# Attention, Fourier mixing and feed-forward on one core: first-half statistics moved up, loads untied, single events shifted by a table

## The chip, the cores and the metric

The kernel runs on one core of a Trainium2 chip. The metric is device time in microseconds (us) from launch to the end of the program. The kernel before has a median of 1042.02 us over three runs (1040.59 to 1042.19). The engines are named as in the profile: PE (TensorE matmul), PEld (its weight loads), DVE (VectorE), ACT (ScalarE), POOL (GpSimd), SP (the engine that issues most DMAs).

## The reference

```python
scores = scale * q @ k^T                       # 8 batches, 8 heads, 576 rows, 64 wide
scores = where(0 <= i - j < 128, scores - slope[h] * |i - j|, -1e9)
attn   = softmax(scores);  x = attn @ v        # heads side by side: 576 x 512 a batch
u      = x + real(fft(fft(x, axis=1), axis=2)) # over the 576 rows and the 512 columns
un     = (u - mean(u)) / sqrt(var(u) + 1e-6)   # over the 512 columns
out    = u + relu(un @ w_ch1) @ w_ch2          # 512 -> 2048 -> 512
```

All is to be right to float32; the two weight matrices come as 8-byte words, which the kernel turns into pairs of float16 itself.

## The kernel before, in words

**Tiling.** The work runs over 32 head pairs p (four a batch). A pair has 576 queries in five tiles, of which each sees one or two blocks of 128 keys; the tiles form three column groups i = 0, 1, 2 (`SGRP`). `products` (L668) makes the scores of a group, with 64-row matmuls of both heads side by side; `spread` adds slope and mask and takes the row minimum on DVE (L684); ACT takes the exponential. In batches 0 and 1 (`NF = 2`) P is turned by PE (`turn`, L715) and multiplied in float32 with v (`values`, L737); from batch 2 on all operands are split in two float16 parts (`convert`, `halves`), P is turned by DMA (`flip`, L706) and each product takes three matmuls (L742 to L744). `weigh` (L756 to L760) divides by the row sums and writes a head's 64 columns of X. There is one `pv` buffer, so a head's `values` wait for the `weigh` of the head before.

**Behind a batch's eight heads** comes `fourier`: rows of X are folded on DVE (L807 to L859), multiplied with cosine tables on PE (`rows` L871, `middle` L888, `cols` L905, three column blocks j in the order 1, 0, 2), and added into X on DVE (`cols_add`, L923 to L934). Then `norm` takes mean and variance (L978, L979), a power on POOL (L981), the shift `nmr` (L983), the normalized rows in two parts (L990, L991 and the difference, L424 `un`), and a DMA transpose into uT. It is called for two halves (X[0:2], X[2:4]) and, for odd batches, a rest. `ffn` is a generator: the first layer (L1151) and relu (L1156), then the second (L1173); each of its `yield`s is one step. The last batch has a variant with fewer products (L1088).

**Beside this** run the weights: loads of 512 KB, two exponent and bit steps (`rebias` L452, `join` L457, L458), a Gram matrix on PE for the scale (L466), and the split into high (ACT, L484) and low (DVE, L488) parts. For batches 2 to 7 `batch_scales` loads q, k and v once more in pieces of up to 256 KB (`fetch`, L528) and squares them on ACT (`part`, L535) for the scale. A one-element POOL copy before the load (L527) reads the X that the last `weigh` wrote, so the load can't go before it; another (L534) ties `part` to the pace of the relu.

**What sets the order.** `put(t, f, ...)` files an event at a time t that is a formula of hand-set numbers (`LB`, `SA`, `F0`, ...). The events run in order of t and emit instructions. `collect` groups these and finds what each waits for, `arrange` plays them through a model with one queue an engine (among the ready ones the first emitted goes first) and `keep_order` writes the resulting order of each engine into the program. So an engine's order is fixed when the program is built.

In the order listings below sp_N are score banks and turned blocks (N is a buffer number), `wall` the weights, `un` the normalized rows. The lines of `norm`'s statistics and of the tie are:

```python
            if b > NF:
                G.tensor_copy(box[x][1][0:1, 0:1], last[-1])   # L527
            nc.sync.dma_start(out=box[x][1], in_=fl[:, o:o + n])  # L528
        for i, t1 in enumerate((t - f * 0.1, t + f * 0.7)):
            put(t1, norm, b, lambda i=i: st["X"][2 * i:2 * i + 2], t + f * (0.9 + 1.6 * i))
```

Of the kernel before, what the change touches and what calls it, by code (L numbers as in the profile page):

```python
# [22 lines left out]
NF = 2  # L23
# [29 lines left out]
SPIN, GAP = 5, 1.315  # L53
# [29 lines left out]
WIDTH = {"float32": 4, "float16": 2, "bfloat16": 2, "int32": 4, "int64": 8}  # L83
LANES = ("PE", "DVE", "Activation", "Pool", "SP")
# [28 lines left out]
def cells(a, seen):  # L113
# [4 lines left out]
    if b.tensor.name[:2] in ("fp", "sp", "pv", "pd"):  # L118
        return b.tensor.name, 0, 128, 1
# [16 lines left out]
def nanoseconds(i, lane):  # L136
# [34 lines left out]
def collect(traced):  # L171
    work, seen, last = [], {}, -1
    for at, i in enumerate(traced):
# [8 lines left out]
        if it is None or bank is None or it.bank != bank or last != at - 1 or len(it.ins) >= 24:  # L182
            it = Work(lane, form, bank)
            work.append(it)
# [10 lines left out]
    writes, reads = {}, {}  # L195
    for n, it in enumerate(work):
        for (t, p0, p1, bits), w in it.uses:
            for l, real in ((writes, True),) + (((reads, False),) if w else ()):
                for m, q0, q1, other in l.get(t, ()):
                    if m != n and q0 < p1 and p0 < q1 and bits & other:  # L200
                        it.waits[m] = it.waits.get(m, False) or real
# [10 lines left out]
def arrange(work, slots):  # L212
# [31 lines left out]
    while len(order) < len(work):  # L244
        best = None
        for e in LANES:
            while now[e] or later[e]:
                t = free[e] if now[e] else max(free[e], later[e][0][0])
                while later[e] and later[e][0][0] <= t:
                    heappush(now[e], heappop(later[e])[1])  # L250
                n = now[e][0]
                t1, tag = buffers(n)
                if t1 is None:
                    held.setdefault(tag, []).append(heappop(now[e]))
                elif t1 > t:
                    ready[n] = max(ready[n], t1)
                    heappush(later[e], (ready[n], heappop(now[e])))
# [5 lines left out]
        n = heappop(now[e])  # L263
# [32 lines left out]
        for m, real in it.then:  # L296
            same = work[m].lane == e
            ready[m] = max(ready[m], end if same and (e == "PE" or not real and e != "SP") else seen + WAKE[work[m].lane])
# [14 lines left out]
def keep_order(tc, slots):  # L313
# [6 lines left out]
    order, takers = arrange(work, slots)  # L320
# [15 lines left out]
def attn_fft_ffn_kernel(  # L336
# [83 lines left out]
    def put(t, f, *a):  # L420
        heappush(queue, (t, next(order), f, a))
# [91 lines left out]
    def batch_scales(b, t0, dt):  # L513
# [6 lines left out]
        def fetch(x, fl, o, n):  # L520
# [5 lines left out]
            if b > NF:  # L526
                G.tensor_copy(box[x][1][0:1, 0:1], last[-1])  # L527
# [263 lines left out]
    def fourier(b, t0):  # L791
# [161 lines left out]
        for j in (1, 0, 2):  # L953
# [10 lines left out]
    def norm(b, of, t1):  # L964
# [7 lines left out]
        uTs[b].append(uT)  # L972
        ag = small.tile([128, 4, 2], F32, name="ag")
        rstd = small.tile([128, 4], F32, name="rstd")
        nmr = small.tile([128, 4], F32, name="nmr")
# [7 lines left out]
        put(t1 - 0.5 * f, lambda: V.scalar_tensor_tensor(nmr[:, :n], ag[:, :n, 0], -1.0, rstd[:, :n], ALU.mult, ALU.mult))  # L983
        uns = {}

        def scaled(i):
            t = t2k.tile([128, 1032], F32, name="un", tag="a4", bufs=3)
            un, both = t[:, 0:512], t[:, 512:1024].bitcast(F16)
            s, o = rstd[:, i:i + 1], nmr[:, i:i + 1]
# [223 lines left out]
    def step(g, t, dt):  # L1213
        if next(g, g) is not g:
            steps[0] += 1
            t += dt + (E0 if steps[0] == 16 else 0.0)
            put(t, step, g, t, dt)

    for b in range(B):
        t = begin_of(4 * b)  # L1220
        if b >= NF:
            batch_scales(b, *((t - SA, SD) if b == NF else (t - SB, SE)))
        fourier(b, transform_of(b))
        n = 80 if b % 2 else 64
        t = forward_of(b)
        put(t, step, ffn(b), t, (24 if b else forward_of(1) - t - E0) / n)
    for f in range(8):
        put(begin_of(4 * B) + 5 + 2.0 * f, combos, f)
    weights(0, W1A, W1D, W1B, W1E)
    weights(1, W2A, W2D, W2B, W2E)  # L1230
    while queue:
        now[0], _, f, a = heappop(queue)
# [115 lines left out]
```

## Time and profile before

| | |
|---|---|
| median of the runs | 1042.02 us |
| the profiled execution | 1041.73 us, its span 1039.9 us |
| PE, DVE, ACT, POOL busy | 1006.7, 761.8, 609.9, 73.3 us |
| mean granted clock of PE | 0.990 |
| DMA | 117.86 MB, mean 113 GB/s, 397 GB/s at most in one of 40 slices |

The page divides the span of 1039.9 us into 40 slices of 26 us. PE is busy 90% or more in nearly all of them; in slices 4 and 5 (78 to 130 us) it has 7 tenths and its granted clock 8 tenths. DVE has 9 and 8 tenths there. The first two slices move 365 and 397 GB/s, and most of the weights. A row with an idle time in brackets names the instruction that ended the engine's wait.

### The profile page before, as it was taken

The page shows a single profiled execution, that of the slowest core. Times are in us where ns is not written, and L with a number is a line of the kernel's source. Part 1 is how long each engine was busy: PE and PEld are TensorE (multiplying, and loading weights), DVE is VectorE, ACT ScalarE, POOL GpSimd, SP SyncE. Part 2 cuts the span into 40 slices and gives each one's busy share as a digit, 9 for nine tenths or more (in the row PEclk, how much of TensorE's full clock was granted, in tenths as well). Part 3 has the DMA queues.
Part 4 walks back from the last instruction along what each step waited for, and adds up shares of the span by engine and source line. Part 5 has one row for each costly group of instructions (what it writes and reads, how often), then busy time and mean ns, then how long its engine had stood idle before and what let it go on. Part 6 is the DMA issues. An engine that isn't in the chain of part 4 may idle for free.

```text
span 1039.9 us, 24569 instructions
## 1 busy us (share of the span) xinstructions
PE 1006.7 (97%) x9352; PEld 730.7 (70%) x9352; DVE 761.8 (73%) x2211; ACT 609.9 (59%) x1438; POOL 73.3 (7%) x243
## 2 busy tenths in 40 slices
PE   8997799899999999999999999999999999999998
PEld 5785585575767677675767677676767776858886
DVE  5898867986784768778784768779684848987451
ACT  7897967676745566567655566667444532445230
POOL 0000001100210012000000012000000000010000
PEclk9998899999999999999999999999999999999999
DMA  9953517656553366534863376434532230011000
GB/s 365 397 187 95 127 34 197 165 105 152 148 135 87 83 154 145 142 77 121 170 136 90 81 157 146 139 80 103 111 93 33 58 70 11 11 35 39 21 3 30
DMA packets 191511, 117.86 MB, mean 113 GB/s; under 512 B 154400, under 2 KB 164128, under 8 KB 191392
## 3 DMA queue, kind: packets, MB, share of 16 engines
q1 hardware_dynamic: 190816, 114.84, 43.9%
q8 instruction: 73, 1.20, 0.5%
q10 hardware_dynamic: 576, 1.45, 0.4%
q14 instruction: 46, 0.38, 0.1%
HBM read 70.63 MB, written 9.44 MB: 77 GB/s over the span
## 4 chain that ended last, share of the span: by engine, by line
PE 66%; DVE 6%; DMA 3%; ACT 2%; issue 1%; POOL 0%; SPq 0%; ACTq 0%; DVEq 0%; POOLq 0%
PE fp L1151 28%; PE fp L1173 25%; PE fp L1088 4%; PE sp L668 3%; DMA pt<-P 2%; PE pd L871 2%; PE pd L905 1%; PE pv L742 1%; PE pv L744 1%; PE pv L743 1%; DVE hbuf L424 1%; DVE P L684 1%; DMA qr<-q_dram 0%; DVE P L424 0%; PE pd L888 0%
## 5 line engine op out<-in xcount | busy, mean ns | idle before, releaser
L1151 PEld LDWEIGHTS <-wall 128*128 128x128 f16 x3840 | 338.8, 98 | 46.2 <-issue 7.9
L1151 PE MATMUL fp<-uT,wall 128*128 128x256 f16 x3072 | 356.1, 273 | 4.5 <-DVE hbuf L424 4.0
L1173 PE MATMUL fp<-wall,hbuf 128*128 128x512 f16 x1536 | 349.1, 379 | 0.7 <-DVE hbuf L424 0.7
L1173 PEld LDWEIGHTS <-hbuf 128*128 128x128 f16 x1536 | 143.6, 98 | 161.0 <-issue 3.1
L1156 ACT ACTIVATE hbuf<-fp 128x512 f16<-128x512 f32 x144 | 85.0, 591 | 186.7 <-PE fp L1151 186.7
L424 DVE SCALAR_TENSOR_TENSOR hbuf<-fp,hbuf 128x512 f16<-128x512 f32 x144 | 98.7, 686 | 95.0 <-ACT hbuf L1156 94.4
L424 ACT ACTIVATE P<-P,nb 128x256 f32<-128x256 f32 x320 | 132.3, 477 | 13.8 <-DVE nb L684 8.2
L684 DVE CUSTOM_DVE_ANT_0 P<-sp,rg,nsl 128x256 f32<-128x256 f32 x240 | 96.2, 448 | 20.8 <-PE sp L668 15.4
L424 DVE SCALAR_TENSOR_TENSOR P<-P 128x256 f16<-128x256 f32 x240 | 83.0, 389 | 22.2 <-ACT P L697 21.6
L697 ACT ACTIVATE P<-P 128x256 f16<-128x256 f32 x240 | 80.7, 385 | 22.4 <-DMA pt<-P 18.7
L668 PE MATMUL sp<-kk,qq 64*128 64x256 f16 (+5 forms) x880 | 77.3, 287 | 4.1 <-DVE kk L424 3.0
L535 ACT ACTIVATE wall<-wall 128x512 f32<-128x512 f32 (+2 forms) x90 | 54.1, 601 | 35.6 <-DMA wall<-k_dram 17.5
L742 PE MATMUL pv<-vhs,pt 128*128 128x65 f16 x432 | 53.9, 195 | 3.9 <-DMA pt<-P 1.9
L743 PE MATMUL pv<-vl,pt 128*128 128x64 f16 x432 | 53.9, 193 | 0.0
L744 PE MATMUL pv<-vhs,pt 128*128 128x65 f16 x432 | 53.8, 193 | 0.0
L742 PEld LDWEIGHTS <-pt 128*128 128x128 f16 x432 | 41.3, 98 | 16.1 <-issue 4.6
L737 PE MATMUL pv<-vr,pt 128*128 128x65 f32 x288 | 40.7, 281 | 5.6 <-DVE X L760 5.1
L743 PEld LDWEIGHTS <-pt 128*128 128x128 f16 x432 | 40.4, 99 | 7.5
L1151 PE MATMUL fp<-wall,wall 128*128 128x128 f16 x768 | 45.0, 219 | 0.0
L737 PEld LDWEIGHTS pv<-vr,pt 128*128 128x128 f32 x288 | 37.9, 200 | 8.8 <-issue 7.1
L668 PEld LDWEIGHTS <-qq 64*128 64x128 f16 (+1 forms) x720 | 31.1, 99 | 15.4 <-issue 11.7
L744 PEld LDWEIGHTS <-pt 128*128 128x128 f16 x432 | 40.6, 97 | 0.0
(230 smaller groups left out, 1380.5 us busy)
## 6 DMA issues: line engine op xcount, KB each, us to landing
qr<-q_dram SPq DMA_DIRECT2D x32, 304.0 KB, 4.0
hbuf<-w_dram SPq DMA_DIRECT2D x16, 512.0 KB, 8.7
out_dram<-X SPq DMA_DIRECT2D x32, 256.0 KB, 2.2
wall<-v_dram SPq DMA_DIRECT2D x30, 256.0 KB, 3.0
vr<-v_dram SPq DMA_DIRECT2D x24, 320.0 KB, 3.7
kr<-k_dram SPq DMA_DIRECT2D x24, 289.0 KB, 4.4
wall<-q_dram SPq DMA_DIRECT2D x24, 256.0 KB, 3.3
wall<-k_dram SPq DMA_DIRECT2D x24, 256.0 KB, 3.0
```

The source lines that it names most:

```text
L424: put(now[0] + dt, lambda: f(*a, **kw))
L535: A.activation(t, t, AF.Square, accum_out=box["mx"][:, i, c:c + 1])
L668: T.matmul(sp[e][:m, col:col + n], qq[h, c0:c0 + m], keys(kk[h], ti), start=(x == 0), stop=(x == len(prods) - 1))
L684: V.tensor_tensor_reduce(pt[:m, 0:n], sp[e][:m, col:col + n], tab[:m, pc:pc + n], mul, 3.0e38, ALU.add, ALU.min, nb[:m, ti:ti + 1])
L697: A.activation(hi, P32, AF.Copy, scale=2.0 ** 14)
L737: T.matmul(pv[:, ti], pt[:, col:col + 128], ops[p][2][:, e, vc], start=first, stop=last)
L742: T.matmul(pv[:, ti], ph, vh[:, e, vc], start=first, stop=False)
L743: T.matmul(pv[:, ti, 0:D], ph, vl[:, e, vc], start=False, stop=False)
L744: T.matmul(pv[:, ti], pl, vh[:, e, vc], start=False, stop=last)
L1151: T.matmul(fp[:, i * n:(i + 1) * n], w1_ap(e, c, f), uT[:, j, c, 0:n], start=(c == 0 and p == 0), stop=(c == 3 and p == 2))
L1156: A.activation(ht[:, 0], fp, AF.Relu)
L1173: T.matmul(op, hh[f][:, a, i * 128:(i + 1) * 128], w2_ap(e, f), start=(f == 0 and p == 0), stop=(f == 15 and p == 2))
```

## The change

Six things. (1) `norm` of the first half is filed behind the second of the three column blocks instead of behind the third, and the times of both halves' scaling get numbers of their own (`N1`, `N2`, `N3`); `nmr` is allocated when it is written. (2) The POOL copy ahead of `fetch` goes, for batches 3 to 7. (3) `arrange` no longer takes the first emitted of the ready ones but the one with the smallest time mark, where the mark is the event's time plus an entry of the table `LATER` (some 80 entries, by the name of the event; plus is later). (4) `collect` also waits where two engines read one PSUM bank, and where instructions of one engine use a tile that another took first. (5) Some 20 of the hand-set numbers move. (6) Feed-forward steps get names, so that the table can speak of them.

```diff
-WL = (-2.569, 0.042)
+WL = (-2.569, -0.036)
-FL, SA, SD, SB, SE = 1.9, 16.181, 0.696, 24.041, 1.166
+FL, SA, SD, SB, SE = 1.9, 16.181, 0.696, 26.459, 1.05
-START = 47.844
+START = 47.9
-SLOW = 1.476
-W2A, W2D, W2B, W2E = 13.895, 0.615, 21.285, 0.518
-W1D, W1B, W1E = 0.379, 11.116, 0.977
-F0 = 5.97
+SLOW = 1.301
+W2A, W2D, W2B, W2E = 14.377, 0.733, 21.018, 0.518
+W1D, W1B, W1E = 0.385, 11.436, 1.124
+F0 = 5.578
+N1, N2, N3 = 1.853, -0.15, 4.606
+LATER = {
+    "W1.load.0": 0.6, "W0.rebias.1": 0.3, "scores.(0,2)+1": 0.15, "W0.gram.2": 1.3, "turn.0.0.0+1": -13.5,
...
+}
-DS, D0 = 1.0, 12
+DS, D0 = 0.505, 12
...
-            for l, real in ((writes, True),) + (((reads, False),) if w else ()):
+            for l, real in ((writes, 2), (reads, 1)):
                 for m, q0, q1, other in l.get(t, ()):
+                    if real == 1 and not w and (work[m].lane == it.lane or t[:2] not in BANKS):
+                        continue
...
-                    heappush(now[e], heappop(later[e])[1])
-                n = now[e][0]
+                    n = heappop(later[e])[1]
+                    heappush(now[e], (rank_of[n], n))
+                n = now[e][0][1]
...
-            if b > NF:
-                G.tensor_copy(box[x][1][0:1, 0:1], last[-1])
             nc.sync.dma_start(out=box[x][1], in_=fl[:, o:o + n])
...
             t += f * 0.8
+            if j < 1:
+                put(t - f * 0.1, norm, b, lambda: st["X"][0:2], t + f * N1)
-        for i, t1 in enumerate((t - f * 0.1, t + f * 0.7)):
-            put(t1, norm, b, lambda i=i: st["X"][2 * i:2 * i + 2], t + f * (0.9 + 1.6 * i))
+        put(t + f * N2, norm, b, lambda: st["X"][2:4], t + f * N3)
...
-        now[0], _, f, a = heappop(queue)
+        now[0], _, here[0], f, a = heappop(queue)
+        marks.append((len(tc.nc.cur_bb.bb.instructions), now[0] + LATER.get(here[0], 0.0), here[0]))
         f(*a)
```

What this does to the orders is shown at three places. The changed kernel's lines stand some 40 further on: its L726 is L684, L532 is L488, L798 to L802 are L756 to L760, L965 to L976 are L923 to L934, L1021 and L1022 are L978 and L979, L468 is the helper L424.

**First place: DVE, around the fold of batch 0, before.** sp_1123 and sp_1124 are the scores of pair 4, group 2; L801 to L859 are the fold, which began nine rows higher up, behind the eighth head's X.

```order
L808 TENSOR_TENSOR fg<-X 128x512
L851 TENSOR_SCALAR stack_104<-pm,sc 33x1
L488 SCALAR_TENSOR_TENSOR wall_109<-wall_109,misc 128x1024
L850 SCALAR_TENSOR_TENSOR stack<-abcd,sc,stack 33x512
L852 SCALAR_TENSOR_TENSOR stack_104<-pm,sc,stack_104 33x1
L684 ISA P,nb<-sp_1123,rel_sb 128x256
L684 ISA nb 128x1
L817 TENSOR_TENSOR pm<-fg 128x2x256
L818 TENSOR_TENSOR pm<-fg 128x2x256
L858 TENSOR_SCALAR a_1054<-pm,sc 128x1
L684 ISA P,nb<-sp_1124,rel_sb 128x256
```

The same scores (here sp_1105 and sp_1106) in the changed order, with the eighth head's X (L802) and the first row of the fold (L843):

```order
L726 ISA P,nb<-sp_1105,rel_sb 128x256
L726 ISA nb 128x1
L726 ISA P,nb<-sp_1106,rel_sb 128x256
L726 ISA nb 128x1
L502 SCALAR_TENSOR_TENSOR wall_110<-X,wall_110 128x512
L532 SCALAR_TENSOR_TENSOR wall_109<-wall_109,misc 128x1024
L798 TENSOR_SCALAR ri<-pv 128x5
L801 RECIPROCAL ri<-ri 128x5
L802 TENSOR_TENSOR X<-pv,ri 128x5x64
L843 MEMSET X 1x512
```

The two spreads stood behind the first part of the fold and now stand ahead of the whole of it. Three weight splits (L488) that stood between X and the fold's last row now stand behind that row.

**Second place: DVE, statistics of batch 0, before,** from the second column block's last addition (L927) on.

```order
L927 TENSOR_TENSOR X<-X,ds 128x512
L978 BN_STATS st<-X 128x6
L923 TENSOR_TENSOR ds<-ab 33x257
L924 TENSOR_TENSOR ds<-ab 33x256
L931 TENSOR_TENSOR ds<-ab 32x257
L930 TENSOR_TENSOR X<-X,ds 1x512
L932 TENSOR_TENSOR ds<-ab 32x255
L933 TENSOR_TENSOR ut<-X,ds 32x512
L934 TENSOR_TENSOR ut<-X,ds 32x512
L979 BN_AGGR ag<-st 128x2
L978 BN_STATS st<-X 128x6 x2
L979 BN_AGGR ag<-st 128x2
```

The same place in the changed order:

```order
L969 TENSOR_TENSOR X<-X,ds 128x512
L1021 BN_STATS st<-X 128x6 x2
L1022 BN_AGGR ag<-st 128x2
L965 TENSOR_TENSOR ds<-ab 33x257
L1022 BN_AGGR ag<-st 128x2
L966 TENSOR_TENSOR ds<-ab 33x256
L1023 TENSOR_SCALAR rstd<-ag 128x2
L973 TENSOR_TENSOR ds<-ab 32x257
L972 TENSOR_TENSOR X<-X,ds 1x512
L974 TENSOR_TENSOR ds<-ab 32x255
L975 TENSOR_TENSOR ut<-X,ds 32x512
L976 TENSOR_TENSOR ut<-X,ds 32x512
```

Both statistics of the first half now stand ahead of the third block, and the second half's, which followed at once, come 26 rows further down.

**Third place: DVE, around the second k split of batch 2's pairs (kk) beside the fold of batch 1, before,** from the seventeenth head's X on.

```order
L760 TENSOR_TENSOR X<-pv,ri 128x5x64
L684 ISA P,nb<-sp_2460,rg,nsl 128x256
L684 ISA nb 128x1
L684 ISA P,nb<-sp_2460,rg,nsl 96x256
L684 ISA nb 96x1
L817 TENSOR_TENSOR pm<-fg 128x2x256
L818 TENSOR_TENSOR pm<-fg 128x2x256
L856 SCALAR_TENSOR_TENSOR fl_2498<-abcd,sc,fh_2455 128x512
L828 TENSOR_TENSOR abcd<-pm 128x2x128 x2
L858 TENSOR_SCALAR a_2500<-pm,sc 128x1
L424 SCALAR_TENSOR_TENSOR vl<-vr,sc,vhs 128x640
L859 SCALAR_TENSOR_TENSOR a_2500<-pm,sc,a_2500 128x1
```

The next row there is the kk split. The same place in the changed order, where sp_2466 is the same group of scores:

```order
L802 TENSOR_TENSOR X<-pv,ri 128x5x64
L726 ISA P,nb<-sp_2466,rg,nsl 96x256
L726 ISA nb 96x1
L468 SCALAR_TENSOR_TENSOR P<-P 128x128
L468 SCALAR_TENSOR_TENSOR kk<-kr,sc,kk 128x578
L468 SCALAR_TENSOR_TENSOR X<-fp,misc,X 128x512
```

Between X and the kk split stood eleven rows, five of them of the fold and one the v split; now there are three, none of them of the fold.

## Rows read from the trace of the kernel before

**Rows 1.** Page: busy us (share) xinstructions.

```profile
PE 1006.7 (97%) x9352; PEld 730.7 (70%) x9352; DVE 761.8 (73%) x2211; ACT 609.9 (59%) x1438; POOL 73.3 (7%) x243
```

**Rows 2.** Stretches: start:end us, busy us (instructions) by engine, PEclk, DMA share, GB/s.

```profile
78.00:84.00 6.00, 1.51 (x4) 0.79 (x4) 5.94 (x16) 3.42 (x7) 0.21 (x2) 0.69 0.00 0
84.00:90.00 6.00, 6.00 (x24) 3.68 (x24) 6.00 (x15) 3.50 (x7) 0.10 (x1) 0.50 0.00 0
...
114.00:120.00 6.00, 3.80 (x18) 3.52 (x19) 5.51 (x21) 6.00 (x10) 0.69 (x1) 0.53 0.44 92
```

**Rows 3.** Timeline of PE: start us, us, operation, [idle before <-what ended it].

```profile
82.01 0.69 PE L715 MATMUL sp<-ident,P 128*128 128x128 f32 x2 [4.03 <-ACT P L424]
...
115.56 1.51 PE L737 MATMUL pv<-vr,pt 128*128 128x65 f32 x6 [4.62 <-DVE X L760]
...
121.66 6.86 PE L1151 MATMUL fp<-uT,wall 128*128 128x256 f16 x48
```

**Rows 4.** Timeline of DVE, 70 to 132 us.

```profile
71.27 0.47 DVE L760 TENSOR_TENSOR X<-pv,ri 128x320 f32<-128x320 f32 x1
...
80.98 0.42 DVE L684 CUSTOM_DVE_ANT_0 P<-sp,rel_sb 128x256 f32<-128x256 f32 x1
81.33 0.08 DVE L684 DVE_READ_ACCUMULATOR2_ANT nb<- 128x1 f32 x1
...
86.47 1.27 DVE L488 SCALAR_TENSOR_TENSOR wall<-wall,misc 128x1024 f16<-128x1024 f32 x1
87.66 0.74 DVE L856 SCALAR_TENSOR_TENSOR fl<-abcd,sc,fh 128x512 f16<-128x512 f32 x1
...
99.63 0.42 DVE L684 CUSTOM_DVE_ANT_0 P<-sp,rel_sb 128x256 f32<-128x256 f32 x1 [2.93 <-PE sp L668]
...
110.92 1.25 DVE L978 BATCH_NORM_STATS2 st<-X 128x6 f32<-128x512 f32 x2
...
116.52 0.69 DVE L424 TENSOR_TENSOR un<-un 128x512 f16<-128x512 f32 x1
```

**Rows 5.** Timeline of PE, 96 to 104 us.

```profile
99.53 0.60 PE L715 MATMUL sp<-ident,P 96*128 96x96 f32 x4
99.98 0.56 PE L737 MATMUL pv<-vr,pt 128*128 128x65 f32 x4
100.37 0.25 PE L580 MATMUL pv<-pt 128*128 128x184 bf16 x1
```

**Rows 6.** Waits of PE from 122 us on: us in total, times, longest.

```profile
PE fp L1151 <- DVE hbuf L424: 4.0, 6, 1.5
PE sp L668 <- DVE kk L424: 3.0, 2, 2.4
PE pv L742 <- DMA pt<-P: 1.9, 2, 1.1
```

**Rows 7.** Timeline of DVE, 185 to 200 us.

```profile
188.77 0.48 DVE L760 TENSOR_TENSOR X<-pv,ri 128x320 f32<-128x320 f32 x1
...
193.56 0.81 DVE L424 SCALAR_TENSOR_TENSOR kk<-kr,sc,kk 128x578 f16<-128x578 f32 x1
```

**Rows 8.** Timeline of PE, 264 to 278 us.

```profile
263.82 2.13 PE L1151 MATMUL fp<-uT,wall 128*128 128x256 f16 x18
265.88 0.88 PE L668 MATMUL sp<-kk,qq 64*128 64x256 f16 x10
...
269.82 5.41 PE L1151 MATMUL fp<-uT,wall 128*128 128x256 f16 x48
275.06 0.19 PE L742 MATMUL pv<-vhs,pt 128*128 128x65 f16 x1
```

**Rows 9.** DMA issues: xcount, KB each, median us to landing; of all issues.

```profile
wall<-v_dram SPq DMA_DIRECT2D x30, 256.0 KB, 3.0
...
pt<-P SPq DMA_TRANSPOSE x240, 2.4
```

**Rows 10.** Waits of SP over the whole span.

```profile
SPq L528 <- POOL wall L527: 52.0, 21, 10.3
```

More of the change, by code (lines that the diff above doesn't have):

```diff
@@ L1 @@
+from bisect import bisect_right
 from contextlib import ExitStack
@@ L183, in collect @@
             it = Work(lane, form, bank)
+            it.at = at
             work.append(it)
@@ L209, in collect, with arrange @@
     return work
-def arrange(work, slots):
+def arrange(work, slots, rank_of):
     left, room, turn, taken, takers, rank = {}, {}, {}, set(), {}, {}
@@ L262, in arrange @@
         s, e = best
-        n = heappop(now[e])
+        n = heappop(now[e])[1]
         it = work[n]
@@ L297, in arrange @@
             same = work[m].lane == e
-            ready[m] = max(ready[m], end if same and (e == "PE" or not real and e != "SP") else seen + WAKE[work[m].lane])
+            at_end = same and (e == "PE" or not real or real == 1 and e != "SP")
+            ready[m] = max(ready[m], end if at_end else seen + WAKE[work[m].lane])
             open_[m] -= 1
@@ L319, in keep_order @@
     work = collect(list(tc.nc.cur_bb.bb.instructions))
-    order, takers = arrange(work, slots)
+    starts = [0] + [m[0] for m in marks]
+    times = [-1.0e9] + [m[1] for m in marks]
+    order, takers = arrange(work, slots, [times[bisect_right(starts, it.at) - 1] for it in work])
     last = {}
@@ L418, in attn_fft_ffn_kernel, with put @@
     now = [0.0]
-    def put(t, f, *a):
-        heappush(queue, (t, next(order), f, a))
+    scope, here, seen, marks = [""], [""], {}, []
+    def put(t, f, *a, name=None):
+        base = here[0] + "+" if here[0] else scope[0] + f.__name__ + "".join(
+            "." + str(x).replace(" ", "") for x in a if type(x) in (int, tuple))
+        base = name or base
+        seen[base] = seen.get(base, 0) + 1
+        key = base + str(seen[base]) if base.endswith("+") else base if seen[base] == 1 else f"{base}#{seen[base]}"
+        heappush(queue, (t, next(order), key, f, a))
     def after(dt, f, *a, **kw):
@@ L972, in norm @@
         uTs[b].append(uT)
+        nmr = []
         ag = small.tile([128, 4, 2], F32, name="ag")
         rstd = small.tile([128, 4], F32, name="rstd")
-        nmr = small.tile([128, 4], F32, name="nmr")
         for i, t in enumerate(tiles):
@@ L982, in norm, with shifts @@
         f = 1 if b else PACE[1]
-        put(t1 - 0.5 * f, lambda: V.scalar_tensor_tensor(nmr[:, :n], ag[:, :n, 0], -1.0, rstd[:, :n], ALU.mult, ALU.mult))
-        uns = {}
+        def shifts():
+            nmr.append(small.tile([128, 4], F32, name="nmr"))
+            V.scalar_tensor_tensor(nmr[0][:, :n], ag[:, :n, 0], -1.0, rstd[:, :n], ALU.mult, ALU.mult)
+        put(t1 - 0.5 * f, shifts)
         def scaled(i):
@@ L1216, in step @@
             t += dt + (E0 if steps[0] == 16 else 0.0)
-            put(t, step, g, t, dt)
+            put(t, step, g, t, dt, name=f"step{steps[0]}")
     for b in range(B):
```

30 lines of the change are left out of this document (20 added, 10 removed), and 19 rows, old and new, of the table LATER.

## The prediction

> **What bounds the kernel now.** I read the page's busy shares first. PE is busy for 1006.7 of 1039.9 us [rows 1], so at most 33 us of idle time can go, and nothing that merely relieves another engine is worth anything unless PE waits for it there. Next the table of stretches. Behind 130 us PE is full nearly everywhere; the hole is at 78 to 126 us, where PE has 1.51 us of work in one six-microsecond stretch and 3.80 in another. There the granted clock is 0.69, 0.50 and 0.53, that is 1.2 GHz for part or all of the stretch, while DVE is busy for 5.94, 6.00 and 5.51 of 6 us [rows 2]. So DVE sets the pace there, and its order decides when PE gets its operands.
>
> The timeline of PE then names the two waits in the hole: 4.03 us for an exponential, 4.62 us for the X of a head [rows 3]. The timeline of DVE says why. The eighth head's X ends at 71.74; the spread whose exponential PE wants starts only at 80.98, behind the first part of the fold and weight splits of 1.27 us; the fold's last row starts at 87.66 [rows 4]. Up to the second `un` at 116.52, on which the first feed-forward matmul at 121.66 hangs [rows 3, 4], DVE has a single gap of note, 2.93 us at 99.63, in which it waits for PE's scores [rows 4]. Last, the waits of PE from 122 us on: the three largest groups add up to 8.9 us, 4.0 for the feed-forward's low part, 3.0 for a k split, 1.9 for transposes of P [rows 6].
>
> The profiled execution took 1041.73 us, 1.83 more than its span and 0.29 less than the median; I work from it and add 0.3 at the end.
>
> **The change part by part.**
>
> *DVE up to the first feed-forward matmul (first and second place).* I compare all DVE rows ahead of the second `un`, before and after, by kind. After the change there are two statistics rows fewer (1.25 us for two [rows 4], 1.2 start to start), one spread fewer (0.35 from start to the next row, 80.98 to 81.33 [rows 4]), two aggregations and nine scalar rows fewer, of `nmr`, of the deviation and of the second weight's scale. Each of these eleven I estimate at 0.07 us, since the shortest DVE row shown takes 0.08. Sum: 1.2 + 0.35 + 0.75 = 2.3 us. The three splits that leave the fold (1.19 each from start to the next row, 86.47 to 87.66 [rows 4]) are not a gain in this sum: they stand ahead of `un` still. But they let the fold end 3 us sooner, so PE's row and column products come sooner, and the splits run while PE does them. The scores that DVE waited 2.93 us for also stand earlier in PE's order. So between nothing and all of that gap closes. The second `un` comes 2.3 to 5.2 us earlier; I take half of the gap, 3.7.
>
> By that moment PE has done more: ahead of the first feed-forward matmul its new order has eight turns more, two `values` instructions more (two records each), a filler matmul and a score matmul more. Four turns take 0.45 us (99.53 to 99.98) and two `values` instructions 0.39 (to 100.37) [rows 5], so 0.9 + 0.4, and 0.3 for the other two (estimate, from the same rows): 1.6 us that need not be done later. This part: 3.9 to 6.8 us, taken at 5.3.
>
> What it does not remove: from the tenth to the eleventh head's X, DVE's rows add up to about 11 us in both orders, by the same durations. So the wait of 4.62 us moves forward but stays, and I leave the stretches at 1.2 GHz as they are. With the cover of DVE's gap gone too, the lower end stands.
>
> *First half's statistics from batch 1 on.* The same rows earlier by a block; the second half's scaling goes from 2.5 to 4.6 units behind the last column block, and the feed-forward's second part needs it some twenty steps later. No PE wait from 122 us on is for a normalized row [rows 6]. Zero; what it might cost sits in the third item's range.
>
> *The k split (third place).* PE waited 2.4 us at most for it [rows 6]; DVE ended X at 189.25 and began kk at 193.56, 4.31 us later [rows 7], eleven rows between. Three rows stand there now. Even if these take 1.5 us the split comes 2.8 earlier, more than the wait. It saves 0 to 2.4; I take 2.4. What is late instead is the fold of batch 1, whose two further rows of work PE now reaches later too.
>
> *All other single shifts.* 8.9 - 2.4 = 6.5 us of waits remain in these groups [rows 6]. I cannot read for each whether it goes, and new ones can come; bounds +6.5 and -6.5. The two waits I could follow through the order both shrink or stay, none grows; I take a third, 2.2.
>
> *Changes between 64-row and 128-row matmuls.* The scores run in 81 separate stretches on PE before, in 76 after. In one place 48 feed-forward matmuls take 269.82 to 275.06, 0.109 each, so 18 take 1.96; yet the scores behind 18 of them start 2.06 later [rows 8]: 0.1 us to enter, and as much to leave again (estimate). Five stretches times 0.2: 1.0 us, between 0.5 and 1.5.
>
> *Loads untied.* 75 POOL copies go. SP waited 52.0 us for them, 21 times, 10.3 at most [rows 10], but nobody's wait on PE hangs on SP except through transposes of P. These land in 2.4 us at the median, a 256 KB load in 3.0 [rows 9]. If transposes pass SP sooner it saves up to the 1.9 us of [rows 6], counted above; if loads crowd them it costs (third rival). Zero.
>
> Sum: 5.3 + 2.4 + 2.2 + 1.0 = 10.9. 1041.7 - 10.9 = 1030.8, and 0.3 for the median: **1031 us**.
>
> **The rivals.**
>
> *1. PE keeps 2.4 GHz.* At 1.2 GHz the three stretches give up 6 x 0.31 + 6 x 0.50 + 6 x 0.47 = 7.7 us of full clock [rows 2], some of it in the waits. Both falls come with a wait of over 4 us [rows 3]. If the shorter DVE queue cuts both waits well below that, up to 7.7 us more come back: 1031 - 7.7 = 1023. For it: the first wait's spread now stands ahead of the fold. Against it: PE, having done these turns, stands next before the scores of pair 5, which are still behind the fold's first part, and the 11 us of DVE rows between two heads remain. The Trainium skill (TensorE: Matmul & The Clock Gate, Part 1) says that the throttled state is the default and activity releases it; the trace agrees in that both falls follow idle time. By that rule the time is this rival's as soon as PE is kept fed.
>
> *2. The saving is given back.* By the thirteenth head's X the DVE rows add up to the same in both orders, so what is done earlier in one place is done later in another; if PE then waits at the second layer's weights, whose low parts end 1.6 us later in the sum of DVE rows, only the lower end of the first item and the switches remain, less new waits of the size of the third: 3.9 + 0.5 - 4 = 0.4 us gained, 1041.6. Against it: after 122 us DVE is seldom full, and PE waited there for the low parts of the feed-forward only 4.0 us in all [rows 6].
>
> *3. Untied loads crowd the transposes (slower).* In SP's order single or grouped loads stand directly ahead of a transpose of P in 20 places, 16 before, one group with five loads. If PE's next `values` is due when such a group is issued, it waits for the loads' share. The price of one such wait is about the 1.1 us that the trace shows as its longest [rows 6]. Today two places show. It decides from ten places on, which cost 11 us and eat the gain; with all 20 it is 22 - 1.9 = 20 us: 1051. For it: the tie was what kept a load behind a head's X. Against it: DMA moves 113 GB/s over the span and 397 in its fullest slice (table of the page's numbers), so there is room, and the load's 3.0 us to land is latency for the most part. The Trainium skill (DMA: Bandwidth & Descriptors, Issuing engines are not separate DMA queues) says that all DMAs run on the same engines and interleave; by that rule crowding costs in every such place, whichever queue issued, and the time is this rival's; no row here shows two of them side by side.
>
> *4. The table does not do on the chip what it does in the planner,* since single shifts of a tenth of a unit are finer than the planner's durations; then the order is another of the same quality: 1042.
>
> **How the numbers follow.** My forecast, 1025 to 1037, has 0.55; the first rival 0.15; the second and fourth together 0.18; the third or another new wait of that size 0.12. The measurement tells 0.2%, about 2 us, from no change. Faster by more, below 1040: the forecast, the first rival and a third of the second and fourth, 0.76. Within: half of those, and some of the third, 0.12. Slower: 0.12. For eight in ten the range goes from 1020, inside the first rival, to 1042, where the second and fourth end; the bounds of the terms, 6.8 + 2.4 + 6.5 + 1.5 = 17 and 3.9 + 0 - 6.5 + 0.5 = -2, give 1025 to 1044 without the clock.
>
> **What would show it.** In the profile after: the spread of pair 4's last group ahead of the fold; the first feed-forward matmul (L1151) at 116 to 119 us instead of 121.66; a wait of 4 to 5 us for a head's X still there, around 107 to 112; stretches at 1.2 GHz still there, together about as long; no wait for kk over 1 us near 190; transposes landing in about 2.4 us. Wrong it would be if the first L1151 comes no earlier than 120, if PE's waits from there on add up to more than 9 us, or if waits for pt<-P pass 5 us.

## The result, and the profile after

The changed kernel took 1029.47 us (median of 4 runs, 1028.22 to 1031.29), the kernel before 1041.91 (1040.59 to 1042.19): ratio 0.9882, 95% interval 0.9865 to 0.9900. Predicted were 1031 us, between 1020 and 1042. The profiled execution took 1028.22 us, so 13.5 us less than that of before.

The page's busy shares show that PE is busy for 1.5 us less than before and, with the span 13.5 us shorter, idle for 21.2 us instead of 33.2; POOL has lost 75 instructions:

```profile
PE 1005.2 (98%) x9352; PEld 731.9 (71%) x9352; DVE 765.3 (75%) x2211; ACT 613.5 (60%) x1438; POOL 49.3 (5%) x168
```

The stretches of the hole (columns as in [rows 2]: PE, PEld, DVE, ACT, POOL busy, then the granted clock):

```profile
78.00:84.00 6.00, 3.35 (x17) 1.52 (x14) 5.97 (x19) 2.50 (x6) 0.21 (x2) 0.73 0.00 0
84.00:90.00 6.00, 5.27 (x32) 3.83 (x31) 5.99 (x20) 4.62 (x11) 0.00 (x0) 0.70 0.00 0
...
102.00:108.00 6.00, 3.97 (x22) 3.01 (x19) 5.85 (x15) 5.62 (x18) 0.93 (x1) 0.72 0.32 81
108.00:114.00 6.00, 4.77 (x23) 3.79 (x21) 5.88 (x27) 6.00 (x15) 0.00 (x0) 0.50 0.44 101
114.00:120.00 6.00, 6.00 (x28) 4.53 (x28) 5.04 (x14) 5.87 (x12) 0.80 (x2) 0.50 0.79 206
```

DVE is about as full as before and the clock is at 1.2 GHz a little longer (24 us against 20.5), but in the first stretch PE has 3.35 us of work instead of 1.51. The timeline of PE there:

```profile
80.58 0.81 PE L757 MATMUL sp<-ident,P 128*128 128x128 f32 x3 [2.08 <-ACT P L468]
...
104.70 0.90 PE L757 MATMUL sp<-ident,P 128*128 128x128 f32 x3 [2.03 <-ACT pt L760]
...
118.18 7.11 PE L1198 MATMUL fp<-uT,wall 128*128 128x256 f16 x48
```

The first feed-forward matmul (L1198, L1151 before) starts 3.5 us earlier. The 4.62 us of [rows 3] for a head's X are gone. Where PE waited 4.03 us for an exponential it now waits 2.08, but for another one. The spreads of pair 4's last scores, which began at 80.98 in [rows 4], stand at 67.78 and 68.12 now, ahead of the fold. What PE waits for at 80.58 is the next exponential, of pair 5's first scores. Its spread stood behind the split (86.47) and the last `fl` (87.66) of [rows 4] before:

```profile
88.80 0.28 DVE L684 CUSTOM_DVE_ANT_0 P<-sp,rel_sb 128x128 f32<-128x128 f32 x1
```

In the changed kernel it stands ahead of both `fl` rows and of the split (84.81), and the second `un` comes at 111.23 instead of 116.52:

```profile
67.78 0.41 DVE L726 CUSTOM_DVE_ANT_0 P<-sp,rel_sb 128x256 f32<-128x256 f32 x1
...
79.80 0.28 DVE L726 CUSTOM_DVE_ANT_0 P<-sp,rel_sb 128x128 f32<-128x128 f32 x1
...
81.88 0.75 DVE L898 SCALAR_TENSOR_TENSOR fl<-abcd,sc,fh 128x512 f16<-128x512 f32 x1
...
84.81 1.28 DVE L532 SCALAR_TENSOR_TENSOR wall<-wall,misc 128x1024 f16<-128x1024 f32 x1
...
111.23 0.69 DVE L468 TENSOR_TENSOR un<-un 128x512 f16<-128x512 f32 x1
```

The waits of PE from 118 us on (total, times, longest) answer to [rows 6]; none is left for a k split, and they add up to 6.8 us. Before, the whole list from 122 us on adds up to 12.7, of which [rows 6] has the three largest groups:

```profile
PE fp L1198 <- DVE hbuf L468: 3.1, 2, 2.0
PE pv L784 <- DMA pt<-P: 1.2, 1, 1.2
PE pd L913 <- DVE zl L921: 1.0, 3, 0.5
PE pv L784 <- DVE X L802: 1.0, 2, 0.6
PE pv L784 <- ACT P L739: 0.5, 1, 0.5
```

**Where the time came from.** I added up PE's matmuls in the order of the trace, each at its length at 2.4 GHz, and read when each profiled execution had done as much work as the kernel before at a given time. The lead in us over the kernel before (labels are those of the experiments below):

| time in before | 120 | 165 | 195 | 225 | 270 | 420 | 510 | end |
|---|---|---|---|---|---|---|---|---|
| after | 6.3 | 5.3 | 10.5 | 8.3 | 11.2 | 10.3 | 14.2 | 13.5 |
| e1 empty table | -1.2 | -1.4 | 0.4 | -2.6 | -0.7 | -2.0 | 1.0 | -0.5 |
| e5 wait gone | -1.0 | -1.0 | -0.7 | -1.1 | -1.5 | -1.0 | 0.0 | -0.3 |
| e7 statistics | -0.4 | 0.4 | 0.6 | 0.0 | 1.3 | 2.4 | 5.2 | 5.6 |
| e8 k split | -1.0 | -1.0 | 1.2 | -0.8 | 0.9 | 2.0 | 1.3 | -0.1 |
| e15 tied, two rows mended | 5.9 | 4.1 | 8.6 | 6.4 | 3.7 | 4.2 | 6.6 | 6.0 |

So 5.3 us are won up to 165 us, 5.2 more up to 195, 2.2 of these given back up to 225 (new waits of 1.25 us for a transpose of P and 1.11 for a low part), and about 6 won again between 225 and 510 us. Of the 8.2 us won behind 165 us, about 5 are idle time of PE; the rest is shorter busy time, which no run separates. The profiled executions of e1 (1042.2 us), e2 (1043.1), e3 (1034.2), e5 (1042.0), e8 (1041.9), e14 (1037.1) and e15 (1035.7) lie 1.4 us or more from their kernel's median, so of those waits and leads in a stretch are read, not totals.

### The profile page after: what moved, and what is told of

The parts are those of the page before. It is cut to its first block, busy times and chain, and to the rows that moved or that the text cites. A ratio compares the mean times of both kernels' runs of the same rounds, so it can differ in the third digit from the quotient of the medians.

```text
span 1026.4 us, 24410 instructions
## 1 busy us (share of the span) xinstructions
PE 1005.2 (98%) x9352; PEld 731.9 (71%) x9352; DVE 765.3 (75%) x2211; ACT 613.5 (60%) x1438; POOL 49.3 (5%) x168
## 4 chain that ended last, share of the span: by engine, by line
PE 77%; DVE 12%; ACT 4%; DMA 4%; issue 1%; SPq 0%; ACTq 0%; DVEq 0%
PE fp L1198 32%; PE fp L1220 26%; PE sp L710 4%; PE fp L1135 4%; DMA pt<-P 2%; PE pd L913 2%; PE pv L779 2%; DVE P L726 2%; PE pd L947 1%; PE pv L784 1%; PE pv L786 1%; DVE wall L532 1%; PE pv L785 1%; PE sp L757 1%; PE pv L622 1%
## 5 line engine op out<-in xcount | busy, mean ns | idle before, releaser
L1198 PEld LDWEIGHTS <-wall 128*128 128x128 f16 x3840 | 339.3, 98 | 43.5 <-issue 4.8
L1198 PE MATMUL fp<-uT,wall 128*128 128x256 f16 x3072 | 355.9, 273 | 3.3 <-DVE hbuf L468 3.1
L468 DVE SCALAR_TENSOR_TENSOR hbuf<-fp,hbuf 128x512 f16<-128x512 f32 x144 | 98.9, 687 | 78.9 <-ACT hbuf L1203 77.7
L468 ACT ACTIVATE P<-P,nb 128x256 f32<-128x256 f32 (+1 forms) x320 | 133.7, 476 | 28.9 <-DVE nb L726 28.0
L726 DVE CUSTOM_DVE_ANT_0 P<-sp,rg,nsl 128x256 f32<-128x256 f32 x240 | 96.1, 452 | 27.6 <-PE sp L710 18.4
L468 DVE SCALAR_TENSOR_TENSOR P<-P 128x256 f16<-128x256 f32 (+1 forms) x240 | 83.1, 390 | 12.2 <-ACT P L739 11.8
L784 PE MATMUL pv<-vhs,pt 128*128 128x65 f16 x432 | 52.9, 195 | 2.7 <-DMA pt<-P 1.2
L786 PE MATMUL pv<-vhs,pt 128*128 128x65 f16 x432 | 52.5, 193 | 0.0
L1198 PE MATMUL fp<-wall,wall 128*128 128x128 f16 x768 | 44.7, 219 | 0.0
L1037 ACT ACTIVATE un<-X,nmr,rstd 128x512 f32<-128x512 f32 x32 | 25.7, 804 | 23.5 <-DVE nmr L1029 21.4
```

What stands on the lines that cost most here:

```text
L468: put(now[0] + dt, lambda: f(*a, **kw))
L726: V.tensor_tensor_reduce(pt[:m, 0:n], sp[e][:m, col:col + n], tab[:m, pc:pc + n], mul, 3.0e38, ALU.add, ALU.min, nb[:m, ti:ti + 1])
L784: T.matmul(pv[:, ti], ph, vh[:, e, vc], start=first, stop=False)
L786: T.matmul(pv[:, ti], pl, vh[:, e, vc], start=False, stop=last)
L1198: T.matmul(fp[:, i * n:(i + 1) * n], w1_ap(e, c, f), uT[:, j, c, 0:n], start=(c == 0 and p == 0), stop=(c == 3 and p == 2))
```

## The experiments

Ratios are to the kernel before, with the 95% interval.

**e1: the table emptied.**

```
-LATER = {"W1.load.0": 0.6, ... 92 more}
+LATER = {}
```

> The changed kernel with an empty table: every event keeps its rank, all else of the change stays (statistics of the first half ahead, loads untied, new hand-set numbers, the planner's finer rules). My theory: the table carries the k split (2.4 us), the spread of pair 4 ahead of the fold, part of the 5.3 us before the first feed-forward matmul (the second un stands at DVE row 314, against 322 before and 307 after), and the small shifts; the matmul-size changes stand at 80 as before. So some 7 to 8 us of the 12.4 go: 1036 to 1038. If the untying or the hand-set numbers carry the gain: 1030, as after. If the table holds other parts of the change in place and their order is bad without it: 1042 or slower.

Measured: 1038.33 us, 0.9968 (0.9952 to 0.9984). The table (it has 93 entries) carries some 9 of the 12.4 us, as expected and a little more. What the other 3 us come from is open: the planner's finer rules and the new numbers have no run of their own. Without it PE waits for the fold where it waited for the exponential before:

```profile
85.14 0.42 PE L892 MATMUL fp<-tab_sb,fh 128*128 128x289 f16 x1 [5.13 <-ACT fh L865]
```

**e14: the first 29 of the 93 entries alone** (to `"values.6.1.0"`, about 160 us).

```
-    "values.6.1.0": 1.5, "f32_scale.1+1": -3.5, ... 63 more
+    "values.6.1.0": 1.5,
```

> The changed kernel with the first 29 of the table's 93 entries alone (up to about 160 us), the rest of the change kept. My theory: the 5.3 us won ahead of and around the first feed-forward matmul stay (order the same up to there), and what follows goes as with an empty table, which gains little more: 1034 to 1037. Rival, the later entries mend little: 1030 to 1032. Rival, without them the early lead is lost again at new waits: 1040.

Measured: 1030.64 us, 0.9898 (0.9877 to 0.9919). My expectation of 1034 to 1037 fell, its first rival held: the early entries are worth about 7.7 us (1038.3 to 1030.6), the other 64 about 1, which the intervals can't tell from nothing. So most of what is won behind 160 us doesn't need the entries that stand there; which of the earlier rows brings it, no run separates. In order, the engines follow the changed kernel up to about 150 us.

**e4: the table kept, the hand-set numbers of before.**

```
-SLOW = 1.301
+SLOW = 1.476
 (and WL, SB, SE, START, GAP, W2*, W1*, F0, DS likewise)
```

> The changed kernel with the hand-set pacing numbers of before (weights' times, START, SLOW, F0, the batch scales, DS); table, statistics and untying stay. My theory: the table's shifts were fitted to the new numbers, so a part of it misses: 64-row and 128-row changes rise to 83 stretches (1.4 us), the second un is back at DVE row 321, so most of the first term goes (3 to 5 us); the k split stays early. 1033 to 1036. Rival, the numbers matter only in the hole and PE has other work: 1030. Rival, the table without its numbers is worse than no table: over 1040.

Measured: 1060.52 us, 1.0168 (1.0145 to 1.0191). The third rival: with other numbers the table is far worse than none. The timeline of PE has the 5 us wait for the fold again, and a new one for the weights' scale:

```profile
86.39 0.42 PE L913 MATMUL fp<-tab_sb,fh 128*128 128x289 f16 x1 [4.97 <-ACT fh L886]
...
125.41 1.51 PE L779 MATMUL pv<-vr,pt 128*128 128x65 f32 x6 [4.18 <-DVE misc L524]
```

**e3: the first half's statistics back behind the third column block** (the second half's go back too, from -0.15 to 0.7; the changed kernel otherwise).

```
-            if j < 1:
-                put(t - f * 0.1, norm, b, lambda: st["X"][0:2], t + f * N1)
...
-        put(t + f * N2, norm, b, lambda: st["X"][2:4], t + f * N3)
+        put(t - f * 0.1, norm, b, lambda: st["X"][0:2], t + f * (N1 - 0.8))
+        put(t + f * 0.7, norm, b, lambda: st["X"][2:4], t + f * N3)
```

> The changed kernel with the statistics of the first two tiles filed behind the third column block again (its scaling keeps its time). My theory: two statistics rows and their aggregation come back in the DVE queue ahead of the second un (row 317 instead of 307), so the first feed-forward matmul comes 1 to 2 us later and the total is 1030 to 1031; nothing from batch 1 on. Rival, the statistics are the heart of the change: 3 to 5 us, 1032 to 1034. Rival, no DVE row in the hole matters since PE has other work there: 1029.5, no change.

Measured: 1029.90 us, 0.9881 (0.9859 to 0.9904): no change. In its profile the first feed-forward matmul starts at 118.97, 0.8 us later than after, and the total doesn't show it.

**e7: the same statistics alone, on the kernel before.**

```
+            if j < 1:
+                put(t - f * 0.1, norm, b, lambda: st["X"][0:2], t + f * 1.7)
...
-        for i, t1 in enumerate((t - f * 0.1, t + f * 0.7)):
-            put(t1, norm, b, lambda i=i: st["X"][2 * i:2 * i + 2], t + f * (0.9 + 1.6 * i))
+        put(t + f * 0.7, norm, b, lambda: st["X"][2:4], t + f * 2.5)
```

> The kernel before with the statistics of the first half (batch 0's first two tiles) ahead of the third column block, nothing else. My theory: the same DVE rows stand earlier, the second un at row 316 instead of 322, so the first feed-forward matmul comes up to 2 us earlier: 1039 to 1042. Rival, this is the heart of the change: 1036 to 1037. Rival, earlier statistics push a spread or an X back in the DVE queue: 1043 or more.

Measured: 1036.22 us, 0.9956 (0.9943 to 0.9969), 4.7 us faster. The size is that of the first rival, the place is not: the first feed-forward matmul stands at 122.07, no earlier than before, and the X wait is 5.79 us. The second transposed tile landed 1.1 us earlier (119.60 against 120.71 us), but PE came to its matmuls late. By the table above the gain comes between 225 and 510 us, most of it behind 420. The timeline of the kernel before has these waits there, and from 470 to 510 us e7 and the changed kernel have none of over 0.4 us:

```profile
475.19 0.19 PE L742 MATMUL pv<-vhs,pt 128*128 128x65 f16 x1 [0.79 <-DVE X L760]
...
506.95 0.20 PE L742 MATMUL pv<-vhs,pt 128*128 128x65 f16 x1 [0.84 <-DMA pt<-P]
...
508.89 5.40 PE L1151 MATMUL fp<-uT,wall 128*128 128x256 f16 x48 [1.49 <-DVE hbuf L424]
```

**e6: pair 4's spread ahead of the fold alone, on the kernel before.**

```
+LATER = {"scores.(4,2)": -2.4, "W0.low.4": 2.2, "W0.low.5": 1.3, "W0.low.6": 0.4}
```

> The kernel before, with the table's machinery and four entries of my own alone: pair 4's last scores ahead of the first part of the fold, three low parts of the weights behind it. Rows of the first place move, little else. My theory: the 4.03 us wait for an exponential at 82 us shrinks to about 2 and PE's work moves forward, but DVE's rows ahead of the second un are not fewer (row 324), so the first feed-forward matmul comes no earlier: 1039 to 1041, 1 to 3 us gained where PE has done more work by then. Rival, this place alone carries the first term: 1036. Rival, the cut wait keeps the clock up and brings more: under 1036.

Measured: 1043.62 us, 1.0025 (1.0016 to 1.0034), slower. The wait for the exponential shrank, and the fold, pushed back, took its place; the normalized rows came late too:

```profile
85.31 0.42 PE L885 MATMUL fp<-tab_sb,fh 128*128 128x289 f16 x1 [5.23 <-ACT fh L858]
...
122.63 8.09 PE L1165 MATMUL fp<-uT,wall 128*128 128x256 f16 x48 [2.18 <-DMA uT<-un]
```

**e8: the k split of pair 10 earlier, alone, on the kernel before.**

```
+LATER = {"convert.10.1+1": -1.2}
```

> The kernel before, with the table's machinery and one entry alone: the k split of pair 10 1.2 units earlier (DVE row 470 instead of 490). My theory: its wait of 2.4 us on PE near 190 us goes and nothing takes its place: 1039 to 1040, 2 us gained. Rival, the gain is given back at the next wait (the fold of batch 1, the low part of the feed-forward): 1041 to 1042.

Measured: 1040.39 us, 0.9989 (0.9977 to 1.0000). That is 0 to 2.4 us, and the interval holds both expectations. The wait for kk of 2.43 us is gone; at the same place PE waits 2.10 us for X's sum, then 1.42 for a transpose. The lead over e5, whose clock fell at the same places, is 1.9 us at 195 and 0.3 at 225, but 2.4 at 270 and 3.0 at 420: what is given back at once is won again later, and most of it is lost behind 420, where the clock fell in this execution near 508. The two waits are:

```profile
194.72 4.09 PE L1165 MATMUL fp<-uT,wall 128*128 128x256 f16 x36 [2.10 <-DVE X L438]
...
205.47 0.20 PE L756 MATMUL pv<-vhs,pt 128*128 128x65 f16 x1 [1.42 <-DMA pt<-P]
```

**e5: the tie's wait taken away, the order of before kept on every engine.**

```
-                G.tensor_copy(box[x][1][0:1, 0:1], last[-1])
+                G.tensor_copy(box[x][1][0:1, 0:1], misc[0:1, 7:8])
 (planned as if it read last[-1])
```

> The kernel before, with one thing changed: the POOL copy ahead of each load reads a constant instead of the latest head's X, so POOL and SP no longer wait there and loads go out as soon as their turn on SP comes; the order on every engine is that of before. My theory: nobody's wait on PE hangs on it: 1041 to 1043, no change; SP's 52 us of waits for POOL shrink or turn into waits for ACT and DVE. Rival, untying is worth its share of the gain: 1036 to 1039. Rival, untied loads crowd the transposes of P: waits for pt<-P rise above 1.9 us and the time to 1044 or more.

Measured: 1039.99 us, 0.9995 (0.9985 to 1.0004). As expected: SP's waits for POOL fall from 52.0 [rows 10] to 28.4 us, and no time that the interval tells from nothing comes of it.

**e2: the ties back in the changed kernel.**

```
+            if b > NF:
+                G.tensor_copy(box[x][1][0:1, 0:1], last[-1])
```

> The changed kernel with the POOL copy back that ties a loaded stretch to the latest head's X (so 75 POOL copies are back, and the planner orders some other rows otherwise too). My theory: loads untied are worth nothing, the transposes of P land as before: 1028 to 1031, the time of after. Rival, the untying brings the gain: towards 1040. Rival, untied loads cost through the transposes: 1024 to 1027, and the 1.25 us wait for pt<-P near 202 us is gone.

Measured: 1041.38 us, 0.9997 (0.9982 to 1.0011): all of the gain is gone, against my theory. For the order of before e5 has shown that the tie's own wait costs nothing. With ties the planner orders much of what stands behind 141 to 148 us otherwise, and the timeline of SP shows what stands badly: two transposes of P behind three of normalized rows, PE waiting 6.25 us for them. In this execution the granted clock also fell at 259.1, for 6.8 us.

```profile
252.44 1.24 SPq L1047 DMA_TRANSPOSE wall<-un  x1
253.76 5.03 SPq L1047 DMA_TRANSPOSE uT<-un  x2
258.89 2.53 SPq L750 DMA_TRANSPOSE pt<-P  x2
```
```profile
262.10 0.24 PE L786 MATMUL pv<-vhs,pt 128*128 128x65 f16 x1 [6.25 <-DMA pt<-P]
```

The timeline of SP in the changed kernel has the same kinds of rows one by one:

```profile
236.38 1.26 SPq L1045 DMA_TRANSPOSE uT<-un  x1
237.74 1.23 SPq L748 DMA_TRANSPOSE pt<-P  x1
239.06 1.26 SPq L1045 DMA_TRANSPOSE wall<-un  x1
240.38 1.24 SPq L748 DMA_TRANSPOSE pt<-P  x1
```

**e15: e2 with these two transposes of P moved ahead of the two of `uT`**, all other orders those of e2.

```
+MOVE = (("SP", "scores.(11,2)+2+2", "F1.norm.1#2+2+2", False),
+        ("SP", "scores.(11,2)+4+2", "F1.norm.1#2+2+2", False))
```

> The changed kernel with the ties back (as in the second experiment), and then two transposes of P near 256 us moved on SP ahead of two transposes of normalized rows; every other engine's order kept. My theory: what the ties cost was no wait for a tie but another order on SP, above all these two rows, for which PE waited 6.25 us: 4 to 6 us back, 1035 to 1037. Rival, the tie's own waits cost: 1041, no change. Rival, the feed-forward's input then comes late by as much: 1039 to 1041, with a wait for uT.

Measured: 1038.27 us, 0.9962 (0.9948 to 0.9976). Against e2 that is 3.1 us by the medians, for two rows on one queue; the intervals are apart. It is less than expected, since PE still waits 4.31 us. SP begins the first of the two transposes at 251.22, but the trace has it landing 5.7 us later, at 256.94, behind three loads and a transpose of normalized rows that SP had issued from 247.74 on and that landed from 251.72 to 256.46. The clock fell here too, at 256.3, for 3.4 us; it did not in the changed kernel. The view of the tile at that time gives issue times in ns and the landing:

```profile
L762 SPq DMA_TRANSPOSE pt<-P x1: 1188/1188/1188, 251.2 to 251.2; - x1
...
DMA to landing us min/median/max: 5.7/5.7/5.7
```
```profile
256.98 0.24 PE L798 MATMUL pv<-vhs,pt 128*128 128x65 f16 x1 [4.31 <-DMA pt<-P]
```

Of the rest of what e2 lost, 2.88 us is a wait of PE for X near 193 us that the changed kernel doesn't have; what else there is was not separated. Whether a table made for the tied kernel would do as well as this one was not tried.

**e11: in the changed kernel, loads behind the transposes in two places.**

```
+MOVE = (("SP", "load.12", "scores.(10,0)+8+2", True),
+        ("SP", "S4.fetch.7.1024.512", "scores.(12,0).(12,1)+16+2", True),
+        ("SP", "load.14", "S4.fetch.7.1024.512", True))
```

> The changed kernel with three rows of SP moved, every other engine's order kept: in two places (near 196 and 260 us) the loads of a later pair that stand directly ahead of transposes of P go behind them. In the changed kernel these loads wait for a split on DVE that frees their buffer, and the transposes wait behind them; DVE then waits 3.25 us near 202 and 2.38 us near 264 for the transposes, and PE 1.25, 1.11 and 1.97 us. My theory: the transposes start 0.5 us (first place) and 2 us (second place) earlier and the waits shrink by as much: 1027 to 1028.5. Rival, the transposes follow one another at 1.5 us each whatever stands ahead: no change, 1029.5. Rival, the loads are late for their own splits: over 1030.

Measured: 1028.36 us, 0.9863 (0.9848 to 0.9878), the lowest median of all, though its interval overlaps that of the changed kernel. In the changed kernel DVE waits for transposes in the first place, with a low part that PE needs (at 203.74) behind them in its queue:

```profile
202.12 0.48 DVE L726 CUSTOM_DVE_ANT_0 P<-sp,rg,nsl 128x256 f32<-128x256 f32 x1 [3.25 <-DMA pt<-P]
```

With the loads behind, DVE waits 1.00 us there and the two waits of PE (1.25 and 1.11) are gone, but not for my reason. The first transpose starts later, at 196.69 instead of 196.21, since SP now waits for P, and lands earlier, at 200.94 instead of 202.10. Behind the two loads it takes 5.9 us to land. The row of the changed kernel, then e11:

```profile
L748 SPq DMA_TRANSPOSE pt<-P x1: 1301/1301/1301, 196.2 to 196.2; - x1
...
DMA to landing us min/median/max: 5.9/5.9/5.9
```
```profile
L761 SPq DMA_TRANSPOSE pt<-P x1: 1190/1190/1190, 196.7 to 196.7; - x1
...
DMA to landing us min/median/max: 4.3/4.3/4.3
```
```profile
200.97 0.48 DVE L739 CUSTOM_DVE_ANT_0 P<-sp,rg,nsl 128x256 f32<-128x256 f32 x1 [1.00 <-DMA pt<-P]
```

In the second place PE's wait stays (2.06 instead of 1.97). The timeline merges seven transposes into one row of 12.56 us there. Each takes 1.2 us to issue (1169 to 1254 ns), as the view of the tile shows; the other 4.1 us are waits of SP between them, 2.7 of them for one P:

```profile
255.63 12.56 SPq L761 DMA_TRANSPOSE pt<-P  x7
```
```profile
L761 SPq DMA_TRANSPOSE pt<-P x7: 1169/1206/1254, 255.6 to 267.0; - x7
...
DMA to landing us min/median/max: 2.3/2.4/6.8
```

The first two, behind loads, landed after 6.8 and 5.8 us, the other five after 2.3 to 2.5. So the waits shrank in one place, as I expected, and no 1.5 us a transpose is seen in the other.

**e13: the same, and the hidden rows ahead of what waits for transposes, on DVE and ACT.**

```
+        ("DVE", "step37+1", "scores.(10,1)", False),
+        ("Activation", "step75", "scores.(12,0).(12,1)+10", False),
+        ("DVE", "step75+1", "scores.(12,0).(12,1)+10+1", False)
```

> As the one before, and on DVE and ACT the low and high part of the feed-forward's hidden rows that PE waits for at 204.5 and 266.8 us go ahead of the spreads and P copies that wait for the transposes. My theory: the two waits of 1.11 and 1.97 us go: 1026 to 1027.5, faster than both kernels. Rival, the P rows pushed back by 0.7 us make PE wait elsewhere: 1029 to 1031.

Measured: 1031.36 us, 0.9899 (0.9884 to 0.9914), slower than e11: the intervals are apart. The wait at 266 us shrank from 2.06 to 1.13, but P rows that were pushed back made others late:

```profile
206.45 0.28 PE L929 MATMUL pd<-tab_sb,fh 128*128 128x289 f16 x1 [0.92 <-DVE zl L937]
...
291.80 0.19 PE L800 MATMUL pv<-vhs,pt 128*128 128x65 f16 x1 [2.92 <-DVE X L818]
```

## Why the prediction was right, and where its steps were not

The time was right to 1.5 us. Of its steps some were right; in the first and largest two errors of opposite sign met, and the other shifts were under-sized.

- **First feed-forward matmul 3.7 us earlier, 5.3 in all.** Right in size, in part by luck: 118.18 against 121.66, and a lead of 5.3 us at 165. The second `un` came 5.3 us earlier, more than the 3.7 I took and just above my upper bound of 5.2. But its transpose landed 5.0 us after it was issued, with a load issued between it and the first one, against 3.2 before; so it was there 3.1 us earlier (117.63 against 120.71), and the matmul follows 0.55 us behind (0.95 before). I counted DVE rows ahead of the second `un` and left the landing out. e3 puts the two statistics and their aggregation back ahead of it and costs 0.8 us there and nothing at the end; e7 moves the statistics alone and gains nothing there. The term needs the table's first entries (e1, e14); the spread and the splits alone do not bring it (e6). Which of the 29 do, no run separates. (The fold before ends with L859 at 88.32, not with the `fl` at 87.66; the sum doesn't use it.)
- **The wait of 4.62 us for X "moves forward but stays".** Wrong: it is gone. DVE's part was right: the tenth and eleventh head's X start at 99.15 and 110.63, 11.5 us apart. But 1.2 GHz takes 24 us in the profile after, 20.5 in that of before (2 us at the very end left out in both), where I had left it as it was, and its second stretch begins at 104.6 instead of 114.4. The two are one thing, as the last section shows: DVE hands out its rows at its own pace, and a slow PE fills the gap that a fast PE waits through.
- **Statistics from batch 1 on: zero.** Failed as a price for the part alone: e7 gains 4.7 us, most of it behind 225 us. I looked for waits for a normalized row, and the waits that went were for other DVE rows (0.79 and 1.49 us) and a transpose. In the changed kernel the part is worth nothing measurable (e3), as the rest removes these waits too.
- **The k split, 2.4 us.** The wait went. Alone it is worth 1.1 us by its ratio, between 0 and 2.4 (e8), and PE then stands at the next wait; the changed kernel has no wait there, and that row stands earlier, too (X's sum at 180.47 instead of 194.42).
- **Other shifts, 2.2 us.** Under-sized. The lead from 165 us to the end grew by 8.2 us, of which I had 5.6 (2.4, 2.2 and 1.0 for fewer changes between 64 and 128 rows). I bounded the term by the three largest groups of waits, 8.9 us; the whole list has 12.7, and 6.8 are left. The scores run in 76 stretches instead of 81, as I said, but what that is worth no run separates.
- **Loads untied, zero.** Right for the wait (e5), wrong as an account: with ties the planner makes another order and the whole gain is gone (e2). A part that "costs nothing" can still decide the order of the others.
- **The rivals.** PE didn't keep 2.4 GHz: the first wait was cut to about 2 us, another of 2.03 stands ahead of where the second was, and the granted clock fell about the end of each, at 80.7 and at 104.6 us. The rule of the Trainium skill (TensorE: Matmul & The Clock Gate, Part 1), that activity releases the throttled state, would have the time at 1023 if PE were kept fed. It wasn't: it had 3.35 and 3.97 us of work in the two six-microsecond stretches in which the clock fell, so the trace doesn't speak against the rule. The fourth, that single shifts act on the chip otherwise than in the planner, is refuted by e1 and e14. The second appears in small (2.2 us given back from 195 to 225). Of the third, that loads crowd the transposes, the crowding is there and the price is not: 14 transposes of P took more than 4.5 us to land in the changed kernel, 11 before, but only once did PE wait for one (1.25 us, and 1.11 for a row behind it), and the two loads ahead of that one, which e11 moves, load q and k of a later pair and were never tied. "There is room" was wrong of the queue: what was issued just ahead counts, not the mean of 113 GB/s. The rule of the Trainium skill (DMA: Bandwidth & Descriptors, Issuing engines are not separate DMA queues), that all DMAs run on the same engines, agrees with the late landings; that every such place costs, as I drew from it, did not come out.

## What to carry to other kernels

Price a reordering as a whole: alone three parts measured 2.7 us slower, 4.7 faster and 0.6 faster by the medians, together with the rest 12.4 faster, and the same table under the old numbers made the kernel 1.7% slower than no change. A wait that is taken away often uncovers the next row of the same queue, so look at what stands there before booking the gain. Where loads and DMA transposes share one queue, put ahead what PE needs next: two rows out of turn cost 3 us here. And before reading a merged row as the price of one instruction, see how much of it is waiting.

## What the runs showed of the hardware

**The price of the half clock depends on who sets the pace.** e5 has the order of the kernel before on every engine. In the profile of before PE ran at 2.4 GHz from 102 to 114 us and then waited 4.62 us for X [rows 3]; in that of e5 the clock had fallen 9 us earlier (105.3 against 114.4). Stretches of before, then of e5:

```profile
102.00:108.00 6.00, 4.55 (x43) 3.95 (x41) 5.97 (x18) 5.41 (x17) 0.20 (x2) 1.00 0.41 132
108.00:114.00 6.00, 2.59 (x17) 1.57 (x15) 5.91 (x25) 4.52 (x14) 0.71 (x1) 1.00 0.70 200
```
```profile
102.00:108.00 6.00, 4.54 (x34) 4.20 (x32) 5.97 (x18) 5.38 (x17) 0.20 (x2) 0.77 0.38 129
108.00:114.00 6.00, 6.00 (x24) 4.33 (x24) 5.91 (x24) 3.64 (x12) 0.71 (x1) 0.50 0.47 139
```

In e5 PE is busy for all of the second stretch at half the clock, and the same matmul then starts at the same time after a wait of 0.46 us; the first feed-forward matmul is 1.0 us later than before (121.66):

```profile
115.59 1.51 PE L744 MATMUL pv<-vr,pt 128*128 128x65 f32 x6 [0.46 <-DVE X L767]
...
122.68 1.68 PE L1159 MATMUL fp<-uT,wall 128*128 128x256 f16 x7
```

So 10 us more at 1.2 GHz, 5 us of full clock, cost 1.0 us, where DVE was full (5.97 and 5.91 of 6 us) in both. Near the start the price is another. e14 has the order of the changed kernel there, but in its profiled execution 6.8 us from 11.7 us on were at 1.2 GHz, and the lead at 30 us is 3.5 us smaller, half of the stretch. The stretch of the changed kernel, then of e14:

```profile
12.00:18.00 6.00, 5.49 (x53) 4.59 (x50) 3.95 (x11) 6.00 (x14) 0.00 (x0) 1.00 1.03 407
```
```profile
12.00:18.00 6.00, 6.00 (x25) 4.00 (x26) 2.57 (x9) 4.09 (x11) 0.00 (x0) 0.50 1.03 401
```

Why the clock fell in one execution and not in another of the same order stays open.

**What SP issued landed in the order of issue.** In the traces of before, after, e2, e11 and e15 none of the 530 transfers on SP landed ahead of one issued before it. The 276 transposes take 1.2 us to issue at the median in each. In the changed kernel 195 of the 240 transposes of P had at most one load or store still under way among the four rows ahead of them, and landed in 2.4 us at the median; the other 45 had more and took 3.7. In the kernel before these are 200 with 2.4 and 40 with 3.5. So a transpose's place among the loads on SP decides when it lands, by up to 4 us in the places above (5.9 and 6.8 us against 2.4).
